# Fillers, later weight steps and a moved factor in a hand-planned kernel

## The chip, the cores and the metric

One Trainium2 chip, one core of it. The metric is the device time of one execution in microseconds; lower is better.

## What is computed

Three stages follow each other: a gated linear attention in chunks, and two feed-forward blocks. Cut to what matters:

```python
# 1. attention: batch 4, 8 heads, 768 steps, head size 32, state size 16
y = (C B^T * decay, causal) @ x  +  decay * (C @ state)          # per chunk
# 2. tokens as rows: 3072 x 256
xn = x / sqrt(mean(x * x) + 1e-6) * rms_g
g = xn @ w_gate; x = (g * sigmoid(g) * (xn @ w_val)) @ w_out     # 256 -> 1536 -> 256
# 3.
h = x @ w_in; solu = h * softmax(h)                              # 256 -> 1024
out = (layernorm(solu) * g_ln) @ w_out2                          # 1024 -> 256
```

All of it is float32. The kernel splits each operand of the large products in a high and a low part of type fp32r and adds three products (high x high, low x high, high x low).

## The kernel before

The 3072 tokens are 24 units `u` of 128 tokens and 6 blocks `b` of four units. A unit goes through the attention; a block through the gated stage in 12 steps `f` of 128 columns; a unit again through the last stage.

**One unit of attention.** TensorE builds the decay matrix for units 0 to 3 (`lpe`, L259; later units load it, L227) and `pcb` = B C (L301). ScalarE takes exponentials (L267), POOL masks (L271), VectorE multiplies both into `L` (L307) and prepares `cd` (L250) and `xb` (`bw`, L231). TensorE makes `y` (old state through L321, the unit's own part L326, new state L331). VectorE copies the state (L340, L342) and spreads it (`sbd`, L348); the next unit's `y` needs it. Then comes the normalisation: ScalarE squares `y` (`sq`, L355) and copies it (`xc`, L389), TensorE sums the squares (`ms`, L361), VectorE scales the sum (`ts`, L374), POOL takes the power -1/2 (`pw`, L379), TensorE spreads the factor over 128 columns of the same PSUM tile (`rb`, L383), VectorE multiplies copy, weight `rms_g` and factor (`xn`, L394), ScalarE makes the high part (`xh`, L401), VectorE the low part (`xl`, L405). A block's first gate product needs the low parts of all its four units.

**One step of the gated stage.** TensorE computes gate and value (`gm`, `vm`, six matmuls each, L558), ScalarE the tanh (L572), VectorE two products (L576, L580), ScalarE the high part `ah` (L586), VectorE or POOL the low part `al` (L592), TensorE adds into the output (`o0`, `o1`, L600).

**Weights.** 26 pieces arrive as 512 KB of 64-bit words (float64 bits). VectorE turns each into float32 in three steps (`wc`, L116, L119, L122); ScalarE makes the high part (`wh`, L129), VectorE or POOL the low part by a subtraction (`w`, L133). Pieces 0 to 17 go, three by three (gate, value, output), to two steps `f` each of block 0.

**What sets the order.** `plan()` places every operation `op(name, engine, us, due, fn, after, new, use)` in one list by rule: for each engine it takes, of the operations that could start within a slack of the earliest, the one that is due first. `us` and due times are written numbers. `new` and `use` count tiles in rings of fixed size, `alt` lets POOL take an operation of VectorE. The engines then run their part of the list in order and wait for each other by semaphores. Accesses of one PSUM tile by different engines are kept in the order of the list. Constants: `PRO` is when block 0 is planned to start, `FIRST` the least length of block 0, `Y0` when the first four units are due and how far apart, `SLACK0` and `SLACK` the slack before and after `PRO + 8`, `CROW` when the cumulated decays are due, `HLAG` how late the last stage of a block is due. Loads are issued by SyncE in the order of the list.

Of the kernel before, what the change touches and what calls it, by code (L numbers as in the profile page):

```python
# [11 lines left out]
AF = mybir.ActivationFunctionType  # L12
ALU = mybir.AluOpType
AX = mybir.AxisListType

P = 128
# [12 lines left out]
PRO = 34.0  # L29
FIRST = 63.0  # L30
VIA_PE = ()
WARM = 7
Y0 = (9.0, 4.0)
YPOS, YSPAN = 0.65, 1.0
TAILGAP = 5.0
SLACK = 0.1
SLACK0 = 0.1
# [3 lines left out]
MARGIN = {"PE": 0.5}  # L41
CROW = 30.0
WGAP = 8.0
HLAG = (50.0, 26.0)
# [7 lines left out]
def fused_kernel(ctx, tc, aT, xbt, bcT, wg, wv, wo1, rg, wi2, wo2, gl, consts, out):  # L52
    nc = tc.nc
    V, A, G, T, S = nc.vector, nc.scalar, nc.gpsimd, nc.tensor, nc.sync
# [143 lines left out]
    st = {}  # L198
# [187 lines left out]
    def at_xc(u):  # L386
        d = st[u]
        d["xts"] = sp.tile([P, 2, P], F32, name="xts", bufs=BUFS["xts"])
        A.activation(d["xts"], d["y"][:, 0:256].rearrange("p (g i) -> p g i", g=2), AF.Copy)  # L389

    def at_xn(u):
        d = st[u]
        for g in range(2):
            V.scalar_tensor_tensor(out=d["xts"][:, g], in0=d["xts"][:, g], scalar=rgt[:, g:g + 1],  # L394
                                   in1=d["y"][:, 384:512], op0=ALU.mult, op1=ALU.mult)
# [222 lines left out]
    ops = {}  # L618
# [70 lines left out]
    for u in range(NU):  # L689
# [62 lines left out]
        op(f"xc{u}", "ACT", 0.42, Y, (at_xc, u), after=[f"y{u}", f"sq{u}"], new=[("xts", f"xt{u}")], use=[f"y{u}", f"xt{u}"])  # L752
        op(f"xn{u}", "DVE", 0.6, Y, (at_xn, u), after=[f"rb{u}", f"xc{u}"], use=[f"y{u}", f"xt{u}"])
# [49 lines left out]
    for u in range(NU):  # L803
        b, k = unit_blk[u]
        n = blk[b][1]
        if b + 1 < NB:
            lag = [HLAG[min(q, 1)] for q in (b, b + 1)]
            H = start[b + 1] + lag[0] + k * (start[b + 2] - start[b + 1] + lag[1] - lag[0]) / n
        else:
            H = start[NB] + 14 + TAILGAP * k  # L810
# [93 lines left out]
    for u in range(2):  # L904
        ops[f"sbd{u}"]["after"].append("cst")
        ops[f"xn{u}"]["after"].append("cst")

    early = [f"lpe{u}.{g}" for u in range(NPE) for g in range(2)] + ["e1p"] + ["cr0", "cr1"]
    ops["wh22"]["after"] += early + ["sf"]

    def plan():
# [48 lines left out]
        while len(order) < len(ops):  # L960
            best = None
            dve = None
            for e, names in ready.items():
                if e == "POOL":
                    names = names + [nm for nm in ready["DVE"] if "alt" in ops[nm] and nm != dve]
                c = [(est(ops[nm], e, MARGIN.get(e, 0.0) if free[e] > PRO else 0.0), nm) for nm in names]
# [14 lines left out]
            if e != o["e"]:  # L981
                o = ops[nm] = dict(o, us=o["alt"][0], fn=o["alt"][1])
                ready["DVE"].remove(nm)
            else:
                ready[e].remove(nm)
            order.append((t, nm))
# [24 lines left out]
    with tc.manual_schedule():  # L1011
# [21 lines left out]
        for _, nm in seq:  # L1033
            fn, *a = ops[nm]["fn"]
            fn(*a)
# [64 lines left out]
```

## Time and profile before

| | |
|---|---|
| time, median of 3 runs | 563.78 us (561.93 to 565.23) |
| the profiled execution | 565.08 us, its span 563.4 us |
| TensorE busy | 546.5 us, 97% of the span |
| VectorE, ScalarE, POOL busy | 390.9, 290.3, 84.8 us |
| chain that ended last | TensorE 81%, VectorE 15%, DMA 2% |

The shares are means over stages. How to read the rows further down: times are microseconds from the start of the span; a matmul of float32 appears as two records; "PEclk" is the granted clock of TensorE as a share of 2.4 GHz (0.50 is 1.2 GHz); "idle before" an instruction is what its engine stood still, with the engine and line that ended it.

### The profile page before, as it was taken

Reading aid. Unit: us, or ns where it says so; the run is one execution under the profiler, and the core shown is the slowest. Engines: PE = TensorE matmul, PEld = TensorE weight load, DVE = VectorE, ACT = ScalarE, POOL = GpSimd, SP = SyncE. Lnnn points to the kernel's source line nnn. Section 1 sums busy time; section 2 is a strip of 40 time slices with the busy share of each in tenths; the row PEclk is TensorE's granted clock in tenths of the full one; section 3 lists DMA queues with packets and bytes.
Section 4 is the critical chain, followed back from the end, with each engine's and each line's share of the span. In section 5 each row is a group of like instructions: output and inputs, shape, how many; then the busy total and the mean of one; then the engine's idle time right before and its main releaser. Section 6 shows DMA issues by size and latency. Waiting matters only on the chain.

```text
span 563.4 us, 9443 instructions
## 1 busy us (share of the span) xinstructions
PE 546.5 (97%) x3544; PEld 461.1 (82%) x3544; DVE 390.9 (69%) x789; ACT 290.3 (52%) x654; POOL 84.8 (15%) x118
## 2 busy tenths in 40 slices
PE   9879998899999999999999999999999999999996
PEld 8757886687888888888888888888888888888795
DVE  5788999999876776575684574684674574564763
ACT  6437654666555564463474454554543353343464
POOL 2333323212221010110111100110100000000010
PEclk9579999999999999999999999999999999999999
DMA  7464765542022021121120220220200000000000
GB/s 213 132 212 140 216 203 194 182 145 71 14 72 76 2 80 47 43 72 36 54 76 11 75 70 10 80 70 10 72 2 9 10 1 9 11 1 10 9 20 30
DMA packets 44366, 39.33 MB, mean 70 GB/s; under 512 B 3936, under 2 KB 36896, under 8 KB 44320
## 3 DMA queue, kind: packets, MB, share of 16 engines
q1 hardware_dynamic: 44320, 38.72, 22.5%
q8 instruction: 28, 0.46, 0.4%
q14 instruction: 18, 0.15, 0.1%
HBM read 35.37 MB, written 3.34 MB: 69 GB/s over the span
## 4 chain that ended last, share of the span: by engine, by line
PE 81%; DVE 15%; DMA 2%; issue 1%; ACT 1%; SPq 0%; POOL 0%; DVEq 0%; ACTq 0%; POOLq 0%
PE pv L558 15%; PE pg L558 15%; PE po L600 14%; PE ph L436 12%; PE pf L538 12%; PE pt L514 4%; PE pcb L301 3%; DVE wt L119 2%; PE y L326 2%; DVE wt L122 2%; DVE th L580 2%; PE y L321 1%; DVE al L592 1%; DVE th L576 1%; DVE L L307 1%; DVE wt L116 1%
## 5 line engine op out<-in xcount | busy, mean ns | idle before, releaser
L586 ACT ACTIVATE ah<-th 128x512 fp32r<-128x512 f32 x72 | 45.2, 628 | 52.2 <-PE po L600 38.8
L580 DVE TENSOR_TENSOR th<-pv,th 128x512 f32<-128x512 f32 x72 | 49.8, 691 | 29.2 <-PE pv L558 24.1
L592 DVE TENSOR_TENSOR al<-th,ah 128x512 fp32r<-128x512 f32 x70 | 49.3, 704 | 26.0 <-ACT ah L586 25.6
L576 DVE SCALAR_TENSOR_TENSOR th<-th,pg 128x512 f32<-128x512 f32 x72 | 49.1, 682 | 20.0 <-ACT th L572 19.7
L558 PE MATMUL pg<-xh,wg_h 128*128 128x512 f32 x144 | 59.5, 413 | 2.3 <-ACT xh L401 1.2
L600 PE MATMUL po<-ah,wo_h 128*128 128x512 f32 x144 | 60.3, 419 | 0.0
L600 PE MATMUL po<-al,wo_h 128*128 128x512 f32 x144 | 56.7, 394 | 2.3 <-DVE al L592 2.3
L558 PE MATMUL pv<-xh,wv_h 128*128 128x512 f32 x144 | 58.4, 406 | 0.0
L558 PE MATMUL pg<-xh,wg_l 128*128 128x512 f32 x144 | 57.0, 396 | 0.0
L558 PE MATMUL pg<-xl,wg_h 128*128 128x512 f32 x144 | 56.8, 394 | 0.0
L600 PE MATMUL po<-ah,wo_l 128*128 128x512 f32 x144 | 56.7, 394 | 0.0
L558 PE MATMUL pv<-xl,wv_h 128*128 128x512 f32 x144 | 56.5, 392 | 0.0
L558 PE MATMUL pv<-xh,wv_l 128*128 128x512 f32 x144 | 56.4, 392 | 0.0
L572 ACT ACTIVATE th<-pg 128x512 f32<-128x512 f32 x72 | 42.6, 592 | 26.6 <-PE pg L558 26.4
L502 POOL TENSOR_TENSOR sc<-sc,mhalf 128x1 f32<-128x1 f32 x24 | 14.1, 587 | 263.6 <-DVE sc L497 263.6
L237 ACT ACTIVATE L<-L,cneg 128x128 f32<-128x128 f32 x160 | 50.5, 390 | 0.6 <-DMA L<-crow 0.6
L460 ACT ACTIVATE ut<-ph,sc 128x1024 f32<-128x1024 f32 x20 | 22.3, 1116 | 54.5 <-DVE sc L447 54.5
L538 PE MATMUL pf<-wo_h,uth 128*128 128x256 f32 x176 | 49.6, 282 | 0.3 <-DVE utl L528 0.2
L538 PE MATMUL pf<-wo_h,utl 128*128 128x256 f32 x176 | 49.6, 282 | 0.0
L538 PE MATMUL pf<-wo_l,uth 128*128 128x256 f32 x176 | 49.5, 281 | 0.0
L447 DVE TENSOR_REDUCE sc<-ph 128x1 f32<-128x1024 f32 x20 | 24.5, 1225 | 31.7 <-PE ph L436 31.7
L523 ACT ACTIVATE uth<-pt 128x512 fp32r<-128x512 f32 x44 | 26.0, 595 | 31.1 <-PE pt L514 30.9
(138 smaller groups left out, 1225.2 us busy)
## 6 DMA issues: line engine op xcount, KB each, us to landing
L<-crow SPq DMA_DIRECT2D x20, 512.0 KB
stage<-in_wo_dram SPq DMA_DIRECT2D x10, 512.0 KB
xb<-in_xbt_dram SPq DMA_DIRECT2D x24, 192.0 KB
stage<-in_wg_dram SPq DMA_DIRECT2D x6, 512.0 KB
bc<-in_bcT_dram SPq DMA_DIRECT2D x48, 64.0 KB
stage<-in_wv_dram SPq DMA_DIRECT2D x6, 512.0 KB
out_dram<-ob SPq DMA_DIRECT2D x24, 128.0 KB
stage<-in_wi_dram SPq DMA_DIRECT2D x4, 512.0 KB
```

Of the source, the lines that this page charges most:

```text
L237: A.activation(d["L"][:, h], d["L"][:, h], AF.Exp, bias=cneg[:, u * 8 + h:u * 8 + h + 1])
L436: T.matmul(ph[c], xx[:, kk, k * P:(k + 1) * P], ww[:, kk, 512 * c:512 * c + 512], start=(i == 0), stop=(i == 5))
L447: V.tensor_reduce(out=sc[:, 0:1], in_=ph[0], axis=AX.X, op=ALU.max, negate=True)
L523: A.activation(d["uT"][0][:, 4 * c:4 * c + 4].rearrange("p k t -> p (k t)"), d["ptc", c], AF.Copy)
L538: T.matmul(d["pf"][:, 0:DM], uu[:, k], ww[:, k], start=(k == 0 and i == 0), stop=(k == 7 and i == 2))
L558: T.matmul(ps[:, :n], ww[:, kk, f * P:(f + 1) * P], xx[:, kk, :n], start=(i == 0), stop=(i == 5))
L572: A.activation(d["th"], d["pg"], AF.Tanh, scale=0.5)
L576: V.scalar_tensor_tensor(out=d["th"], in0=d["th"], scalar=1.0, in1=d["pg"], op0=ALU.add, op1=ALU.mult)
L580: V.tensor_tensor(out=d["th"], in0=d["pv"], in1=d["th"], op=ALU.mult)
L586: A.activation(d["ah"], d["th"], AF.Copy)
L592: e.tensor_tensor(out=d["al"], in0=d["th"], in1=d["ah"].bitcast(F32), op=ALU.subtract)
L600: T.matmul(po[b, m][:, :n], ww[:, f, m * P:(m + 1) * P], aa, start=(f == 0 and i == 0), stop=(f == NF - 1 and i == 2))
```

## The change

Three edits of code and seven of constants. `xc` takes the weight `rms_g` as the scale of ScalarE's copy, in two instructions, one for each half (each half has its own weight column); `xn` becomes one product of 128x256 on VectorE, and waits no longer for the weight's load, `xc` does. In the planner, TensorE's margin (an operation of another engine counts as ready that much later) becomes a function `mg`: weight operations get a margin of 1.0 us on every engine (names that begin with `w` but for `wd`), TensorE's others keep 0.5 after `PRO`. And `warm` puts matmuls of the constant `ones` into 62 unused columns of the last `y` tile wherever TensorE is planned to be idle for over 0.5 us before `PRO + 6`, in a number that fills 70% of that time. The constants move the due times, so the whole list is ordered anew.

```diff
-PRO = 34.0
-FIRST = 63.0
+PRO = 28.0
+FIRST = 70.0
-Y0 = (9.0, 4.0)
+Y0 = (9.0, 3.5)
-SLACK = 0.1
-SLACK0 = 0.1
+SLACK = 0.05
+SLACK0 = 0.2
-CROW = 30.0
+CROW = 20.0
-HLAG = (50.0, 26.0)
+HLAG = (40.0, 26.0, 1)
+WMG = 1.0
+FILL = 0.7
...
     def at_xc(u):
         d["xts"] = sp.tile([P, 2, P], F32, name="xts", bufs=BUFS["xts"])
-        A.activation(d["xts"], d["y"][:, 0:256].rearrange("p (g i) -> p g i", g=2), AF.Copy)
+        for g in range(2):
+            A.activation(d["xts"][:, g], d["y"][:, g * P:(g + 1) * P], AF.Copy, scale=rgt[:, g:g + 1])
     def at_xn(u):
-        for g in range(2):
-            V.scalar_tensor_tensor(out=d["xts"][:, g], in0=d["xts"][:, g], scalar=rgt[:, g:g + 1],
-                                   in1=d["y"][:, 384:512], op0=ALU.mult, op1=ALU.mult)
+        V.tensor_tensor(out=d["xts"], in0=d["xts"], in1=d["y"][:, 384:512].unsqueeze(1).to_broadcast([P, 2, P]), op=ALU.mult)
...
+    def warm(u, n):
+        if u not in st:
+            return
+        for _ in range(n):
+            T.matmul(st[u]["y"][:, 322:384], ones, ones[:, 0:62], start=True, stop=True, skip_group_check=True)
...
+        def mg(nm, e):
+            if nm[0] == "w" and nm[1] != "d":
+                return WMG
+            return MARGIN.get(e, 0.0) if free[e] > PRO else 0.0
...
-                c = [(est(ops[nm], e, MARGIN.get(e, 0.0) if free[e] > PRO else 0.0), nm) for nm in names]
+                c = [(est(ops[nm], e, mg(nm, e)), nm) for nm in names]
...
+            if e == "PE" and lasty is not None and t < PRO + 6 and t - free[e] > 0.5:
+                order.append((free[e], (warm, lasty, int((t - free[e]) * FILL / 0.22))))
```

The planned `us` of `xc` and `xn` change places (0.42 and 0.6). The formula around `HLAG` gives 40 for block 0 and 26 for the others, where it gave 50 and 26.

In the rows of order below each line is an instruction (line, operation, output<-inputs, shape); lines of the changed kernel are numbered anew. ScalarE behind the exponentials of unit 1, before:

```order
L267 ACTIVATE L<-pv,cneg 128x128 x4
L129 ACTIVATE wv_h<-wt 128x2x256
L355 ACTIVATE sq<-y 128x256
L389 ACTIVATE xts<-y 128x256
L267 ACTIVATE L<-pg,cneg 128x128 x4
```

and now:

```order
L269 ACTIVATE L<-pv,cneg 128x128 x4
L357 ACTIVATE sq<-y 128x256
L392 ACTIVATE xts<-y,rgt 128x128 x2
L269 ACTIVATE L<-pg,cneg 128x128 x4
L269 ACTIVATE L<-pv,cneg 128x128 x4
L402 ACTIVATE xh<-xts 128x2x128
L357 ACTIVATE sq<-y 128x256
L392 ACTIVATE xts<-y,rgt 128x128 x2
L131 ACTIVATE wv_h<-wt 128x2x256
```

The high part `wv_h` of weight piece 1 moved from ahead of unit 0's square to behind unit 1's copies.

TensorE from the fourth unit's `y` to block 0's first product, before (the first `rb` is unit 2's):

```order
L326 MATMUL y<-L,xb 32x128 x8
L331 MATMUL y<-xb 32x64 x4
L383 MATMUL y<-ident,r 128x128
L361 MATMUL y<-ones,sq 128x1 x2
L383 MATMUL y<-ident,r 128x128
L558 MATMUL pg<-xh,wg_h 128x512
```

and now:

```order
L328 MATMUL y<-L,xb 32x128 x8
L333 MATMUL y<-xb 32x64 x4
L917 MATMUL y<-ones 128x62 x2
L363 MATMUL y<-ones,sq 128x1 x2
L917 MATMUL y<-ones 128x62 x4
L385 MATMUL y<-ident,r 128x128
L559 MATMUL pg<-xh,wg_h 128x512
```

Unit 2's `rb` moved ahead of this piece; the two groups of L917 are all the fillers of the program.

VectorE from unit 3's scaled sum to its low part, before:

```order
L374 TENSOR_SCALAR r<-y 128x1
L122 SCALAR_TENSOR_TENSOR wt<-stage,wt 128x512
L116 TENSOR_SCALAR wt<-stage 128x512
L119 SCALAR_TENSOR_TENSOR wt<-stage,wt 128x512
L394 SCALAR_TENSOR_TENSOR xts<-xts,rgt,y 128x128 x2
L133 TENSOR_TENSOR wv_l<-wt,wv_h 128x2x256
L405 TENSOR_TENSOR xl<-xts,xh 128x2x128
```

and now:

```order
L376 TENSOR_SCALAR r<-y 128x1
L118 TENSOR_SCALAR wt<-stage 128x512
L121 SCALAR_TENSOR_TENSOR wt<-stage,wt 128x512
L124 SCALAR_TENSOR_TENSOR wt<-stage,wt 128x512
L396 TENSOR_TENSOR xts<-xts,y 128x256
L135 TENSOR_TENSOR wg_l<-wt,wg_h 128x2x256
L406 TENSOR_TENSOR xl<-xts,xh 128x2x128
```

Before, the steps between were the last of piece 4 and two of piece 5; now they are the three of piece 4, and the subtraction is piece 3's.

## Rows read from the trace of the kernel before

**Rows 1.** Chain of waits, 9 to 48 us: start, us, engine, what, line.

```profile
7.96 4.25 DMA cd<-in_bcT_dram
...
13.35 1.06 DVE wt L119
...
15.16 0.03 ACT wv_h L129
...
16.36 0.24 DVE s L340
...
17.66 1.92 PE pv L259 x8
...
22.06 2.01 PE pcb L301 x16
...
40.22 2.96 PE pg L558 x6
```

**Rows 2.** Stretches, TensorE alone: from:to, length, busy, clock, DMA share, GB/s.

```profile
16.00:17.00 1.00, 0.36 (x2) 0.82 0.67 120
30.00:30.50 0.50, 0.50 (x20) 0.71 0.00 0
37.00:38.00 1.00, 0.00 (x0) 0.56 1.05 402
43.50:44.00 0.50, 0.50 (x3) 0.55 1.05 331
```

**Rows 3.** Timeline of the prologue: start, us, engine, line, operation, idle before.

```profile
10.77 1.06 PE L259 MATMUL pv<-um,la 128*128 128x128 f32 x8
...
11.99 1.16 ACT L267 ACTIVATE L<-pv,cneg 128x128 f32<-128x128 f32 x4
...
16.64 1.01 PE L361 MATMUL y<-ones,sq 128*128 128x1 f32 x4 [1.95 <-DVE s L340]
...
21.21 0.44 PE L331 MATMUL y<-xb 128*32 128x64 f32 x8
...
30.27 0.30 PE L331 MATMUL y<-xb 128*32 128x64 f32 x8
...
34.49 0.29 PE L331 MATMUL y<-xb 128*32 128x64 f32 x6
...
35.61 0.60 PE L361 MATMUL y<-ones,sq 128*128 128x1 f32 x4 [0.58 <-ACT xts L389]
```

**Rows 4.** Groups by shape: count, then busy us, mean ns, idle before.

```profile
L119 DVE SCALAR_TENSOR_TENSOR wt<-stage,wt 128x512 int32<-128x512 int32 x26 | 19.5, 749 | 0.5
L394 DVE SCALAR_TENSOR_TENSOR xts<-xts,rgt,y 128x128 f32<-128x128 f32 x48 | 14.4, 341 | 6.3 <-PE y L383 6.2
L405 DVE TENSOR_TENSOR xl<-xts,xh 128x256 fp32r<-128x256 f32 x24 | 10.4, 435 | 2.9 <-ACT xh L401 2.8
L133 DVE TENSOR_TENSOR wg_l<-wt,wg_h 128x512 fp32r<-128x512 f32 x3 | 2.0, 682 | 0.0
L379 POOL TENSOR_TENSOR r<-r,mhalf 128x1 f32<-128x1 f32 x24 | 14.7, 614 | 78.2 <-DVE r L374 70.2 <-DMA xb<-in_xbt_dram 8.0
L389 ACT ACTIVATE xts<-y 128x256 f32<-128x256 f32 x24 | 9.2, 382 | 8.8 <-DVE s L342 6.2 <-DVE s L340 2.5
```

**Rows 5.** Stretch of 10 us: busy of PE, PEld, DVE, ACT, POOL, then clock.

```profile
100.00:110.00 10.00, 9.50 (x53) 7.31 (x51) 9.90 (x22) 5.86 (x15) 1.51 (x2) 1.00 0.74 231
```

**Rows 6.** Timeline of TensorE, 84 to 150 us, with idle before in brackets.

```profile
95.75 0.50 PE L600 MATMUL po<-al,wo_h 128*128 128x512 f32 x1 [1.84 <-DVE al L592]
...
106.72 0.50 PE L600 MATMUL po<-al,wo_h 128*128 128x512 f32 x1 [0.49 <-DVE al L592]
...
111.87 0.50 PE L558 MATMUL pg<-xh,wg_h 128*128 128x512 f32 x1 [0.98 <-DVE th L576]
...
135.53 0.35 PE L361 MATMUL y<-ones,sq 128*128 128x1 f32 x2 [0.20 <-DVE sq L369]
```

**Rows 7.** Timeline of VectorE: the tenth low part of block 0.

```profile
95.02 0.68 DVE L592 TENSOR_TENSOR al<-th,ah 128x512 fp32r<-128x512 f32 x1
```

More of the change, by code (lines that the diff above doesn't have):

```diff
@@ L751, in fused_kernel @@
         op(f"rb{u}", "PE", 0.12, Y, (at_rb, u), after=[f"pw{u}"], use=[f"y{u}"])
-        op(f"xc{u}", "ACT", 0.42, Y, (at_xc, u), after=[f"y{u}", f"sq{u}"], new=[("xts", f"xt{u}")], use=[f"y{u}", f"xt{u}"])
-        op(f"xn{u}", "DVE", 0.6, Y, (at_xn, u), after=[f"rb{u}", f"xc{u}"], use=[f"y{u}", f"xt{u}"])
+        op(f"xc{u}", "ACT", 0.6, Y, (at_xc, u), after=[f"y{u}", f"sq{u}"], new=[("xts", f"xt{u}")], use=[f"y{u}", f"xt{u}"])
+        op(f"xn{u}", "DVE", 0.42, Y, (at_xn, u), after=[f"rb{u}", f"xc{u}"], use=[f"y{u}", f"xt{u}"])
         op(f"xh{u}", "ACT", 0.42, Y, (at_xh, u), after=[f"xn{u}"] + ([f"xh{u-1}"] if k else []), new=[("xs", f"xs{b}")] if k == 0 else [],
@@ L806, in fused_kernel @@
         if b + 1 < NB:
-            lag = [HLAG[min(q, 1)] for q in (b, b + 1)]
+            lag = [HLAG[0] + (HLAG[1] - HLAG[0]) * min(1.0, q / HLAG[2]) for q in (b, b + 1)]
             H = start[b + 1] + lag[0] + k * (start[b + 2] - start[b + 1] + lag[1] - lag[0]) / n
@@ L905, in fused_kernel @@
         ops[f"sbd{u}"]["after"].append("cst")
-        ops[f"xn{u}"]["after"].append("cst")
+        ops[f"xc{u}"]["after"].append("cst")
     early = [f"lpe{u}.{g}" for u in range(NPE) for g in range(2)] + ["e1p"] + ["cr0", "cr1"]
     ops["wh22"]["after"] += early + ["sf"]
+    def warm(u, n):
[3 more added lines that the diff above has]
+            T.matmul(st[u]["y"][:, 322:384], ones, ones[:, 0:62], start=True, stop=True, skip_group_check=True)
     def plan():
@@ L958, in est @@
             return t
-        while len(order) < len(ops):
+        def mg(nm, e):
+            if nm[0] == "w" and nm[1] != "d":
+                return WMG
+            return MARGIN.get(e, 0.0) if free[e] > PRO else 0.0
+        lasty = None
+        while len(end) < len(ops):
             best = None
@@ L985, in plan @@
                 ready[e].remove(nm)
+            if nm[0] == "y":
+                lasty = int(nm[1:])
+            if e == "PE" and lasty is not None and t < PRO + 6 and t - free[e] > 0.5:
+                order.append((free[e], (warm, lasty, int((t - free[e]) * FILL / 0.22))))
             order.append((t, nm))
@@ L1033, in fused_kernel @@
         for _, nm in seq:
-            fn, *a = ops[nm]["fn"]
+            fn, *a = ops[nm]["fn"] if isinstance(nm, str) else nm
             fn(*a)
```

## Prediction

> **What bounds the kernel now.** I read the busy time by stretches first, then the chain of waits up to block 0, then the timeline of TensorE. The reader should see three stages. Late in the span TensorE is the bound (97% busy over all), and nothing in the change touches a matmul there; the last 140 TensorE entries stand in the same order in both programs. Up to 40.22 us four units of attention run one after the other, and block 0's first product can only start behind the fourth [rows 1]. Between, from about 45 to 140 us, VectorE is the tight engine: in 100 to 110 us it is busy 9.90 of 10 us, TensorE 9.50 [rows 5]. TensorE's waits in that stage are 1.84, 0.49, 0.98 and 0.20 us, together 3.51, the first three for VectorE [rows 6]. So an earlier block 0 is worth only what VectorE, with its weight steps, can follow.
>
> The chain to 40.22 us has two faults [rows 1]. First, a load of `cd` takes 4.25 us to land behind a weight piece, VectorE stands for it, and then ScalarE's `wv_h` at 15.16 us stands ahead of unit 0's square; the squared sum of unit 0 (L361) comes at 16.64 us only [rows 3]. Second, TensorE's clock. It was idle for 1.95 us ahead of that, from 14.7 us [rows 3], and within 16 to 17 us the granted clock falls from 2.4 to 1.2 GHz; it comes back at 30.3 us. It falls again within 37 to 38 us and is back within 43.5 to 44 us [rows 2]. At 1.2 GHz the eight matmul records of L259 take 1.92 us and the sixteen of `pcb` 2.01 us [rows 1]; at 2.4 GHz the same eight took 1.06 us [rows 3].
>
> **The change, part by part: the prologue.** I walk unit by unit through the new order with the durations of the rows, at 2.4 GHz.
> Unit 0 to 1: `y` of unit 0 now stands ahead of unit 1's `pcb`, so it starts when L259 ends at 10.77 + 1.06 = 11.8 us [rows 3] and has its eight products and four state matmuls through by 12.6. VectorE's part before it is shorter, since unit 1's `bw` and `cd` go to POOL (whose next work waits for ScalarE until 12.1 anyway) and `cd`'s load is issued ahead of `wv`'s. ScalarE is busy with exponentials until 11.99 + 1.16 = 13.15 us [rows 3]; then square and the two weighted copies follow at once, `wv_h` later. The square costs a like step, 0.3. The copy was one instruction of 0.38 us [rows 4]; two of 128x128 cost a step of 0.26 (from the four in 1.16 us: three steps and one of 0.38) and 0.38, so 0.64, or 0.26 more per unit. L361 can start at 14.1 instead of 16.64 and takes 0.6 [rows 3]; two L259 groups of 1.0, the transposed factor 0.3 and `y` of unit 1 with 1.3 follow: it ends near 18.3, against 21.65 before [rows 3].
> Unit 1 to 2: the state copy behind a conversion step (0.75, L119 [rows 4]), square and copies 0.9, L361 0.6, two L259 groups 2.0, factor 0.3, `y` 1.3, handoffs 0.3: 24.4, against 30.57 [rows 3].
> Unit 2 to 3: copy, square and copies 1.7, L361 0.6, two `L` products on VectorE 1.4 (0.68 each, as L133 of that size [rows 4]), `y`'s products 1.1: 29.2, against 34.78 [rows 3].
> Unit 3 to block 0: state copy and ScalarE's three until 30.8. Here stand the fillers, the only six in the whole program. They write the tile `y` that VectorE and ScalarE read, so the first two wait for those reads and run behind the gap, not in it. A filler is bounded below by a 64-column matmul record (0.29 us for six, so 0.1 per filler with its two records) and above by L361, which has the same weight load: 0.60 for two matmuls, 0.3 each, doubled at 1.2 GHz [rows 3]. I take 0.25, nearest to L361. Two: 0.5, so L361 ends at 31.9 instead of 31.4; VectorE would be in a conversion step until then anyhow. The four before the factor: 1.0, beside POOL's 0.61 [rows 4] and beside three steps of weight piece 4, which now stand on VectorE between the sum and the factor's use (none over the 0.75 of L119, the first about 0.4: 1.9). Those steps set that place: 34.0; the fillers cost nothing under this cover at 2.4 GHz, and up to 0.7 at 1.2. Then the product 0.44, ScalarE's copy 0.42: block 0 starts near 35.2, against 40.22: **5.0 us earlier**. I keep 4 to 6 for it.
> The product itself was two instructions of 0.341 [rows 4] and is now one of 128x256; nearest is L405 of that shape, 0.435 [rows 4]: 0.25 less per unit on VectorE. In return ScalarE has 0.26 more; from unit 4 on it is covered, as ScalarE is busy 5.86 of 10 us [rows 5].
> The gap ahead of block 0 stays (29.2 to 35.2, with few matmuls), so I expect its first products at 1.2 GHz again, six in 2.96 us [rows 1]; nothing is won or lost there.
>
> **VectorE takes most of it back.** Counting the two orders up to the end of block 0's first `al`, the new one has done less: one piece's conversion (1.9), two `cd` and one `bw` products (about 1.0), four units' weighting (4 x 0.25), but one subtraction more (0.68): 3.1 to 3.2 us less by then. So of the 5.0 only 1.9 is idle time of VectorE saved. Up to the tenth `al` the lists hold the same work but for: subtractions of weights 12 instead of 8 (POOL takes four fewer), 4 x 0.682 = 2.7 more [rows 4]; seven units' weighting, 7 x 0.25 = 1.7 less; one `cd` product, 0.3 less. Together 0.7 more. The tenth `al` ended at 95.02 + 0.68 = 95.7 us [rows 7], the moment at which TensorE's 1.84 us wait ends [rows 6]. In the new order it ends at 95.7 + 0.7 - 1.9 = 94.5. TensorE, 5 us ahead, waits there some 4 us in all, in pieces from about 68 us on, as each subtraction of weight pieces 7 to 16 comes close behind its use. At that place it has one unit's attention matmuls more behind it (`pcb` 1.0, half of 2.01 [rows 1], and 1.6 for the rest) and six gate products fewer (half of 2.96 [rows 1]): 1.1 us of work more. So 1.2 + 1.1 = 2.3 us are won by then. The three later waits of before (1.67 us [rows 6]) should mostly go, for TensorE then trails VectorE by more; and POOL's four fewer subtractions leave VectorE freer (an L119 beside POOL took 1.05 us [rows 1] against the mean of 0.749 [rows 4]). I add 1.5 for both. **Sum: 3.8 us less.** The weight loads keep pace: piece 7's load now stands behind two 512 KB loads of `L`, but its first step stands at about 46 us, some 2 us behind where I put its landing; were it later, TensorE would lose as much.
>
> The profiled execution took 565.08 us, span 563.4 and 1.7 around it; it lies 1.3 above the median of the runs, 563.78. 565.1 - 3.8 = 561.3, and 1.3 lower for a median: **560.0**.
>
> **A rule against the trace.** The granted clock fell in the gap after 14.7 us, and again within 37 to 38 us although L361's four records had run at 35.61 us, after 0.58 us of idling [rows 2, 3]; so those few short matmuls did not hold it. The Trainium skill (TensorE: Matmul & The Clock Gate, section "HAM oscillation — how this bites in real kernels") puts the fall on waits between groups of matmuls that let the array go cold; read strictly, matmuls in the gap would keep 2.4 GHz. By the row the fillers do nothing, and the sum is as above; by the rule block 0 starts at full clock, which is rival C.
>
> **Rivals.**
> A, no change: the clock falls in the new prologue too. TensorE still idles there about 0.5 us at 13.6 and 1.0 at 19.2 (`pcb` done, ScalarE not). If one of these does it, L259, `y`, `pcb` and L361 of two units double: 4 to 5 us, block 0 at 40. VectorE idles 4.5 us longer than in my walk, so the tenth `al` ends at 99, 3.3 later than before; 1.1 of work ahead and the 1.5 come off, 0.7 are left: 564.5. For it: a gap of 1.95 did it before; against: these are shorter. Chance 0.19.
> B, slower: the same fall, but the clock does not come back before block 0 (before it needed until 30.3, and the new prologue has shorter dense stretches). Then unit 3's `y`, L361, the cumulated decays' matmuls and the fillers double too, 3 us more: block 0 near 43, the tenth `al` at 102, all of it behind rival A: 567.5. It decides when block 0 starts later than about 42. Chance 0.09.
> C, the fillers do hold the clock: six products take 1.5 instead of 2.96 and three more follow; VectorE has conversions as cover, so up to 1.8 us: 558.2. This is also the change doing what it says; my forecast says that six fillers behind their waits don't. Chance 0.07.
> D, VectorE follows: with POOL off its back its steps shrink and the 5.0 us come through whole, later waits included: 565.1 - 5.0 - 1.5 - 1.3 = 557.3. For it: L119's mean of 0.749 is 0.07 over L133 of the same size; against: 9.90 of 10 us busy. Chance 0.12.
> The forecast keeps 0.53, itself 558 to 562.5 by the 4 to 6 us and the 1.5 either way.
>
> **How the numbers follow.** 0.5% is 2.8 us, about what a measurement of this kernel can tell from no change; faster means below 561.0. Of the forecast's 0.53 I give 0.38 to that side, with C and D 0.57. Within 0.5%: 0.15 + 0.17 of A = 0.32; slower: B and the rest of A, 0.11. The range leaves out B and the lowest of D: 556.2 to 565.4.
>
> **What would show it.** Right: unit 1's square ahead of `wv_h`, L361 of unit 0 near 14.1 us, clock 2.4 GHz throughout 14 to 29 us, block 0's first product at 34 to 36.5 us and slow; the tenth `al` at 93 to 96 us; TensorE's waits from 65 to 95 us up to about 4 us, and few after. Wrong: a granted clock of 1.2 GHz before 29 us (A, B), fillers between the fourth `y` and its sum with a fast first product (C), no wait on VectorE from 65 to 95 us (D), or a first product past 38 us at full clock, which would mean that my walk misses a wait.

## The result, and the profile after

The changed kernel takes **565.68 us** (median of 20 runs, 564.05 to 568.91); the kernel before, run beside it, 563.77 (560.80 to 565.46). The ratio is 1.0052, with a 95% interval of 1.0034 to 1.0069: slower by half a per cent, 1.9 us. The forecast was 560.0 with a range up to 565.4, so it was wrong in size and in sign.

The profiled execution took 565.36 us, span 563.6, which is level with the one of before (565.08, span 563.4). It lies 0.3 below its median; that of before lay 1.3 above its own. A comparison of the two traces alone would read "no change".

TensorE's timeline of the prologue, after (start, us, engine, line, operation, idle before it), answers to [rows 3]:

```profile
13.45 0.61 PE L363 MATMUL y<-ones,sq 128*128 128x1 f32 x4 [0.18 <-ACT xts L392]
...
18.27 0.29 PE L333 MATMUL y<-xb 128*32 128x64 f32 x8
...
21.55 0.60 PE L363 MATMUL y<-ones,sq 128*128 128x1 f32 x4 [1.89 <-ACT xts L392]
22.02 2.05 PE L261 MATMUL pg<-um,la 128*128 128x128 f32 x8
23.86 1.81 PE L261 MATMUL pv<-um,la 128*128 128x128 f32 x8
...
33.49 0.66 PE L917 MATMUL y<-ones 128*128 128x62 f32 x4 [2.06 <-ACT xts L392]
33.99 0.56 PE L363 MATMUL y<-ones,sq 128*128 128x1 f32 x4
34.87 1.26 PE L917 MATMUL y<-ones 128*128 128x62 f32 x8 [0.32 <-DVE r L376]
35.92 0.42 PE L385 MATMUL y<-ident,r 128*128 128x128 f32 x1
38.04 0.79 PE L559 MATMUL pg<-xh,wg_h 128*128 128x512 f32 x1 [1.70 <-ACT xh L402]
```

The reader is to see that the front of the prologue goes as the walk said (unit 0's sum at 13.45, unit 1's `y` done at 18.56), and that from there it loses. Unit 1's sum waits 1.89 us, the two L261 groups behind it take 2.05 and 1.81 instead of 1.1 each, and the fillers (L917) run behind their waits. Block 0 starts at 38.04, against 40.22 [rows 1]: 2.2 us earlier, not 5.0.

The granted clock of the stretches in which it falls or rises, after, answers to [rows 2] (from:to, length, then busy time of PE, PEld, DVE, ACT and POOL, granted clock, DMA share, GB/s):

```profile
21.00:22.00 1.00, 0.45 (x4) 0.45 (x5) 0.83 (x2) 1.00 (x3) 0.00 (x0) 1.00 0.88 180
22.00:23.00 1.00, 1.00 (x6) 1.00 (x6) 0.74 (x3) 0.01 (x1) 0.49 (x1) 0.51 0.57 147
25.00:26.00 1.00, 1.00 (x9) 1.00 (x8) 0.18 (x1) 0.54 (x3) 0.63 (x1) 0.79 0.06 16
35.00:36.00 1.00, 1.00 (x9) 1.00 (x9) 0.88 (x2) 0.00 (x0) 0.88 (x2) 0.83 0.95 312
42.00:43.00 1.00, 1.00 (x5) 0.73 (x4) 0.36 (x1) 0.15 (x1) 0.00 (x0) 0.75 0.98 379
```

TensorE goes from 2.4 to 1.2 GHz within 22 to 23 us, behind the idle 1.89 us, and is back within 25 to 26; it falls again within 35 to 36, behind the idle 2.06 us and while the fillers run, and is back within 42 to 43.

The chain of waits of after, 12 to 40 us, names what came ahead of unit 1's sum and of unit 3's normalisation (start, us, what):

```profile
12.23 5.76 DMA xb<-in_xbt_dram
...
18.01 0.77 DVE xb L233
18.78 0.33 DVE xts L396
...
31.95 2.92 DMA cd<-in_bcT_dram
...
35.09 0.44 DVE wt L118
35.55 0.89 DVE wt L121
36.46 0.69 DVE wt L124
37.15 0.34 DVE xts L396
```

The chain gives a load the whole time from issue to landing; what VectorE stood still for it, its timeline says:

```profile
14.54 0.43 DVE L118 TENSOR_SCALAR wt<-stage 128x512 int32<-128x512 int32 x1 [1.62 <-DMA stage<-in_wv_dram]
...
18.01 0.77 DVE L233 TENSOR_TENSOR xb<-xb,wdec 128x128 f32<-128x128 f32 x1 [0.46 <-DMA xb<-in_xbt_dram]
...
20.29 0.27 DVE L344 SCALAR_TENSOR_TENSOR s<-s,e,y 128x64 f32<-128x64 f32 x1
```

The load of `xb` takes 5.76 us to land, but VectorE stands only 0.46 us for it, and 1.62 us earlier on for the load of weight piece 1. Then the weighting (L233), unit 0's product (L396), a `cd` product and two conversion steps run before unit 1's state copy (L344), although unit 1's `y` was done at 18.56. The second load of the chain, at 31.95, held VectorE for 0.27 us (before the step at 35.09); the three conversion steps of weight piece 4 then run ahead of unit 3's normalisation.

VectorE's tenth low part of block 0 and the wait of TensorE on it, after, answer to [rows 6, 7]:

```profile
96.97 0.68 DVE L593 TENSOR_TENSOR al<-th,ah 128x512 fp32r<-128x512 f32 x1
...
97.71 0.51 PE L601 MATMUL po<-al,wo_h 128*128 128x512 f32 x1 [1.49 <-DVE al L593]
```

It ends at 97.65 us, 1.95 **later** than before, although block 0 started 2.2 earlier. And TensorE, from block 0's first product to the end, as one stretch with the same columns, before:

```profile
40.22:563.40 523.18, 513.41 (x3258) 431.33 (x3258) 363.95 (x726) 270.84 (x600) 71.10 (x95) 1.00 0.20 62
```

and after:

```profile
38.04:563.60 525.56, 514.86 (x3258) 431.88 (x3258) 364.85 (x719) 278.30 (x621) 63.08 (x85) 0.99 0.20 61
```

Busy time is +1.45 us and idle time 10.70 against 9.77, so +0.93: together 2.4, which is the 2.2 won by the start and 0.2 more. About 0.4 of the 1.45 is the clock: ten products of block 0 run 0.43 us apart here before the clock is back, and eight before, where 0.23 is usual later.

**A ledger of VectorE.** Since the tenth low part is where the forecast put its sum, I add up VectorE's timeline to its end: *idle* is time between steps; *stretch* is time by which a step lasts longer than is usual for its operation and shape (the lower quartile over the traces of this case; counted where it is over 0.08 us); *work* is the rest. Stretch and work depend on that choice of the usual length by up to 0.4 us; idle does not.

| | ends | idle | stretch | work |
|---|---|---|---|---|
| before, tenth `al` | 95.70 | 15.54 | 3.99 | 76.17 |
| after, tenth `al` | 97.65 | 16.27 | 5.29 | 76.09 |
| before, fifteenth | 125.03 | 16.21 | 3.99 | 104.83 |
| after, fifteenth | 129.59 | 16.88 | 6.24 | 106.47 |

The forecast had work +0.7, idle -1.9 and no row for stretch. To the tenth `al` work came as -0.1, idle as +0.7 and stretch as +1.3: of the error of 3.15 us idle is 2.6 and stretch 1.3, and work takes 0.8 back.

### The profile page after: what moved, and what is told of

It is laid out like the page before. It is cut to its first block, busy times and chain, and to the rows that moved or that the text cites. A ratio compares the mean times of both kernels' runs of the same rounds, so it can differ in the third digit from the quotient of the medians.

```text
span 563.6 us, 9460 instructions
## 1 busy us (share of the span) xinstructions
PE 544.1 (97%) x3556; PEld 458.1 (81%) x3556; DVE 390.2 (69%) x774; ACT 298.1 (53%) x678; POOL 76.4 (14%) x109
## 4 chain that ended last, share of the span: by engine, by line
PE 76%; DVE 17%; issue 2%; DMA 2%; POOL 1%; ACT 1%; DVEq 0%; POOLq 0%; ACTq 0%
PE pv L559 14%; PE pg L559 14%; PE po L601 14%; PE pf L539 12%; PE ph L437 11%; PE pt L515 4%; PE pcb L303 3%; DVE wt L121 2%; DVE th L581 2%; DVE al L593 2%; DVE th L577 2%; PE y L328 2%; DVE wt L124 2%; DVE wt L118 2%; DVE L L309 1%
## 5 line engine op out<-in xcount | busy, mean ns | idle before, releaser
L471 DVE SCALAR_TENSOR_TENSOR ut<-ph,ut 128x1024 f32<-128x1024 f32 x20 | 24.5, 1225 | 23.9 <-ACT ut L461 23.9
```

Of the source, the lines that this page charges most:

```text
L471: V.scalar_tensor_tensor(out=d["u"], in0=ph[0], scalar=1.0, in1=d["u"], op0=ALU.mult, op1=ALU.mult, accum_out=sc[:, 2:3])
```

## The experiments

**Theories.** Theory 1: VectorE's list sets the pace to about 140 us, so an earlier block 0 is worth only what VectorE's idle time shrinks by. Theory 2: TensorE's clock in the prologue sets the time. Theory 3: one part of the change has a price of its own. A fourth came up on the way: VectorE's stretched steps are held up by POOL.

### One part at a time

No fillers:

```
-FILL = 0.7
+FILL = 0.0
```

> The changed kernel without its six filler products, all else as it is. In the profiled execution of the changed kernel the fillers stood at 33.49 us (0.66) and 34.87 us (1.26), both behind a wait, so unit 3's factor came about 1 us later than it could. Theory 1 (VectorE's list paces up to about 140 us): block 0 starts up to 1 us earlier (first product near 37) but the time stays at 565.0 to 565.9 us, ratio 1.002 to 1.004. Theory 2 (the clock's falls in the prologue set the time): without fillers the clock falls no more and no less, so 565 to 566 too, or up to 1 us worse if the fillers did hold it in some executions. Theory 3 (one part has its own price, here the fillers): back by the 1 us that they cost or more, 563.8 to 564.7.

566.19 us, ratio 1.0047 (1.0024 to 1.0069). The six fillers neither cost nor give anything that can be measured; in its profile block 0 started at 38.96 and the clock fell in the prologue too (0.50 from 20 to 24 us).

The weight in ScalarE's copy alone, on the kernel before:

```
-        A.activation(d["xts"], d["y"][:, 0:256].rearrange(...), AF.Copy)
+        for g in range(2):
+            A.activation(d["xts"][:, g], d["y"][:, g * P:(g + 1) * P], AF.Copy, scale=rgt[:, g:g + 1])
...
+        V.tensor_tensor(out=d["xts"], in0=d["xts"], in1=d["y"][:, 384:512].unsqueeze(1).to_broadcast(...), op=ALU.mult)
```

> The kernel before with only the weight moved into ScalarE's copy (two copies with a scale, one product on VectorE instead of two); all lists in their old order. VectorE saves about 0.27 us per unit (two steps of 0.341 against one of 0.41). Theory 1: seven units lie ahead of 100 us, 1.7 to 1.9 us less on VectorE, and its waits shrink by about that: 562 to 563 us, ratio 0.9965 to 0.9985. Theory 2: the clock's falls are not touched (the gap of 1.95 us ahead of unit 0's squared sum stays): 563.8, ratio 0.999 to 1.001. Theory 3, that this part is the one with the price: ScalarE's second copy lengthens each unit's chain by 0.25 us, 564.5 to 566.

563.80 us, ratio 0.9999 (0.9978 to 1.0019). VectorE did 1.7 us less work up to the tenth `al` (74.44 against 76.17), as costed, and nothing that can be measured reached the end; theory 1's gain of 0.15 to 0.35% is at best its small end.

The converse, the changed kernel with the old copy and products:

> The changed kernel with the copy and the two products on VectorE of before (the list as in the changed kernel). VectorE has 0.27 us more per unit, seven units by 100 us: theory 1 expects the tenth al 1.5 to 1.9 later and 566.5 to 567.5 us. Rival (the weight in the copy gives nothing, as on the kernel before alone, 563.8): 565.3 to 566.

565.46 us, ratio 1.0038 (1.0017 to 1.0059). The rival came true: this part is worth nothing that can be measured, on either list.

The margin on weight steps alone, on the kernel before:

```
+        def mg(nm, e):
+            if nm[0] == "w" and nm[1] != "d":
+                return 1.0
+            return MARGIN.get(e, 0.0) if free[e] > PRO else 0.0
...
-                c = [(est(ops[nm], e, MARGIN.get(e, 0.0) if free[e] > PRO else 0.0), nm) for nm in names]
+                c = [(est(ops[nm], e, mg(nm, e)), nm) for nm in names]
```

> The kernel before with only the margin of 1 us on the readiness of weight steps in the planner; constants, copies and products as before. VectorE makes two subtractions more (16 instead of 14; POOL's is the rest of 23). Theory 1: 2 x 0.68 = 1.4 us more on VectorE up to the end of the weights, less what a rarer stall behind a load gives: 564 to 565.5, ratio 1.000 to 1.003. Theory 2: nothing, 563.8. Theory 3, that this part is the one with the price: the whole 1.9 us, 565 to 566.5.

**568.75 us**, ratio 1.0093 (1.0062 to 1.0125): 5 us slower, far more than either theory had, and that with block 0 starting at 36.59, 3.6 us *earlier* than in the profile of before. This run refuted two things at once, that an early block 0 is a gain by itself and that the clock is the price (mean granted clock of the profiled execution 0.991, before 0.981). The groups by shape of VectorE between 45 and 140 us show where it went (count, then busy us, mean ns, idle before); before first:

```profile
L119 DVE SCALAR_TENSOR_TENSOR wt<-stage,wt 128x512 int32<-128x512 int32 x19 | 14.3, 751 | 0.2
L122 DVE SCALAR_TENSOR_TENSOR wt<-stage,wt 128x512 int32<-128x512 int32 x19 | 14.0, 735 | 0.3
```

and with the margin alone:

```profile
L122 DVE SCALAR_TENSOR_TENSOR wt<-stage,wt 128x512 int32<-128x512 int32 x20 | 17.8, 888 | 0.2
L119 DVE SCALAR_TENSOR_TENSOR wt<-stage,wt 128x512 int32<-128x512 int32 x20 | 17.0, 850 | 0.4
```

The same steps on the same data last 100 to 150 ns longer in the mean. By the ledger to the fifteenth `al` (134.72, before 125.03): idle -0.2, work +3.9 (its list has more weight steps ahead of that place), stretch 9.97 against 3.99, +6.0. (The trace has 17 subtractions on VectorE instead of 13, four more and not the two that were expected.)

Margin and copy with the old constants and without fillers:

```
-PRO = 28.0
+PRO = 34.0
...
-FILL = 0.7
+FILL = 0.0
```

(`FIRST`, `Y0`, `SLACK`, `SLACK0`, `CROW` and `HLAG` go back in the same way.)

> The changed kernel with the planner's constants of before (start of block 0, its length, first unit, slacks, row of the decays, lag) and no fillers, so margin on weights and weight in the copy alone. VectorE makes 21 subtractions here, as in the changed kernel (before 14). Theory 1: 7 x 0.68 = 4.8 us more and 16 x 0.27 = 4.3 less on VectorE: near before, 563.5 to 565. Theory 2: depends on the clock: with a fall ahead of 20 us as before, 564 to 566; without it 562 to 563. Theory 3, that the constants are the part with the price: 563.5 or less.

564.54 us, ratio 1.0014 (0.9993 to 1.0035). Theory 1's number came out; theory 3's 563.5 lies at the edge of the interval. With the copy's new costs the planner makes quite another list of the same margin, with a stretch of 4.63 to the fifteenth `al` instead of 9.97: so the margin has no fixed price; it seems to lie in the list that falls out of it.

### Is it the number of subtractions on VectorE?

By the traces the changed kernel makes 19 of its 22 subtractions of weight pieces on VectorE, the kernel before 13; POOL does the others. Six of them given to POOL in the changed kernel, then to VectorE in the kernel before, the order of both lists kept:

```
+        for i in (1, 3, 8, 9, 15, 20):
+            ops[f"w{i}"]["fn"] = (w_lo, i, G)      # in the other run V
```

> The changed kernel with the subtractions of weight pieces 1, 3, 8, 9, 15 and 20 on POOL, as in the kernel before, instead of on VectorE; the list else the same. That takes 6 x 0.68 = 4.1 us off VectorE, four of the six ahead of the tenth al, and gives POOL steps of some 1.2 us. Theory 1 (what VectorE has to do up to about 140 us sets the time, so the seven subtractions that moved to it are the price): the tenth al ends 1.5 to 2.7 us earlier than 97.65, the median falls to 563.5 to 564.5. Rival (the price is in the order of the list, not in VectorE's work): 565 to 566.5, with TensorE waiting for POOL's late subtractions.

569.81 us, ratio 1.0104 (1.0069 to 1.0138): wrong way round for theory 1. The tenth `al` ends at 100.53: work -2.3, but stretch +2.4 and idle +2.9. Its steps beside subtractions on POOL hold 3.7 us of the stretch, where in the changed kernel they hold 0.9.

> The kernel before with the same six subtractions on VectorE instead of POOL; the list else the same. Theory 1: 4.1 us more on VectorE up to 110 us, less what POOL's slower step kept others waiting: the tenth al 1.5 to 2.7 us later than 95.70, the median 565.3 to 567. Rival (the order is the price, not VectorE's work): 563.5 to 564.5.

564.25 us, ratio 1.0016 (1.0001 to 1.0031). Five more subtractions ahead of the tenth `al` make 2.75 us more work, and it ends only 0.42 later: stretch fell from 3.99 to 2.16 and idle by 0.5. A subtraction on POOL can come back as stretch, then, as in the run before; here, though, none of the eight subtractions that POOL makes ahead of the tenth `al` of the kernel before stretched a step, and what fell away (3.8 to 1.9 us) is stretch beside POOL's selects (the masking of `L`), which met other VectorE steps in the shifted list. My form of theory 1, by which VectorE's instruction count is the price, fell here.

### POOL holds VectorE up

One place of many, in the kernel before: the timeline of VectorE,

```profile
65.64 1.59 DVE L122 SCALAR_TENSOR_TENSOR wt<-stage,wt 128x512 int32<-128x512 int32 x1
```

and that of POOL:

```profile
65.36 1.32 POOL L241 TENSOR_SCALAR_AFFINE_SELECT L<-L 128x1024 f32<-128x1024 f32 x1 [2.55 <-ACT L L237]
```

POOL's step runs to 66.68. The conversion that started inside it lasts 1.59 instead of 0.68 us: 0.91 more, and 1.04 of it lay beside POOL. It looks held until POOL is done and then runs nearly its usual time (0.55 us). Two runs test that, with 24 products of a constant on POOL that nobody needs, and with as much of POOL's time in fills that read nothing:

```
+            if nm in DUMMY:               # second conversion step of pieces 7 to 18
+                for _ in range(2):
+                    G.tensor_tensor(out=scr, in0=um, in1=um, op=ALU.mult)
...
+                for _ in range(5):        # the control
+                    G.memset(scr, 1.0)
```

> The kernel before with 24 products on POOL that nobody needs (128x384 of a constant in SBUF, written to a tile of their own; two behind the second conversion step of each of the weight pieces 7 to 18), all else the same. New theory (POOL holds up VectorE): in the trace of before the VectorE steps that read two SBUF tensors, or convert from SBUF, last up to 1.6 instead of 0.7 us where they start beside a long POOL step; the sixteen long POOL steps between 45 and 140 us stretch them by 3.7 us in all, 0.23 each. 24 more of about 1 us then cost 4 to 6 us of VectorE and, as VectorE sets the pace, 567 to 570 us. Rival (VectorE's order and waits are the price, POOL's company is harmless): 563.5 to 565.

**573.88 us**, ratio 1.0188 (1.0158 to 1.0218): 10.6 us slower, more than expected. The tenth `al` ends at 104.83, 9.1 later: idle 15.33, work 75.99, both as before, and stretch 13.51 against 3.99.

> The control: the same places, but POOL only fills the tile with a constant (five fills of 128x384 at each place instead of two products), reading nothing from SBUF. New theory: the two-tensor steps of VectorE are not held up; what is left is that POOL's own steps come up to 2 us later: 563.5 to 565.5 us. If POOL's being busy at all were the price (its own steps coming late), this would cost as much as the products, 567 or more.

562.54 us, ratio 1.0001 (0.9977 to 1.0025): nothing, though POOL was busy as long. The same three VectorE steps stand beside the products and beside the fills. With the products, the timeline of VectorE:

```profile
61.77 0.41 DVE L116 TENSOR_SCALAR wt<-stage 128x512 int32<-128x512 int32 x1
62.10 1.31 DVE L592 TENSOR_TENSOR al<-th,ah 128x512 fp32r<-128x512 f32 x1
63.34 1.31 DVE L119 SCALAR_TENSOR_TENSOR wt<-stage,wt 128x512 int32<-128x512 int32 x1
```

and POOL beside them:

```profile
61.77 2.33 POOL L1040 TENSOR_TENSOR scr<-um 128x384 f32<-128x384 f32 x2
```

With the fills, VectorE:

```profile
56.67 0.69 DVE L116 TENSOR_SCALAR wt<-stage 128x512 int32<-128x512 int32 x1
57.28 0.67 DVE L592 TENSOR_TENSOR al<-th,ah 128x512 fp32r<-128x512 f32 x1
57.88 0.68 DVE L119 SCALAR_TENSOR_TENSOR wt<-stage,wt 128x512 int32<-128x512 int32 x1
```

and POOL:

```profile
56.66 2.49 POOL L1040 MEMSET scr<- 128x384 f32 x5
```

Steps that take two tensors from SBUF are held by POOL's reads (1.31 against 0.67 and 0.68) and not by its fills; the conversion's first step, with one tensor, is held by fills that started just ahead of it (0.69 against 0.41). It is held by selects as well. In the changed kernel, VectorE:

```profile
64.92 1.32 DVE L118 TENSOR_SCALAR wt<-stage 128x512 int32<-128x512 int32 x1
```

and POOL:

```profile
64.66 1.29 POOL L243 TENSOR_SCALAR_AFFINE_SELECT L<-L 128x1024 f32<-128x1024 f32 x1 [4.25 <-DMA stage<-in_wo_dram]
```

Over the 18 traces, 33 of the 34 such first steps that started inside a select lasted longer. Steps that take one operand from PSUM kept their length: none of the 980 that started inside a POOL step lasted longer by over 0.08 us. One of them in the kernel before, beside a subtraction of 1.30 us on POOL from 91.00:

```profile
91.03 0.68 DVE L576 SCALAR_TENSOR_TENSOR th<-th,pg 128x512 f32<-128x512 f32 x1
```

The Trainium skill says this in "SBUF — State Buffer", section "Who interferes with whom": VectorE and GpSimd share a port pair that one instruction holds whole, and a VectorE instruction with two SBUF inputs meets it against a GpSimd instruction that reads SBUF, not against one that only writes. These runs agree for steps with two tensors (1.31 against 0.67 and 0.68). The held one-tensor step (1.32 instead of 0.42) is beyond what that rule says.

### How much of it is the clock

Fillers that run in the gaps, on a tile that nobody reads any more, in the changed kernel and in the kernel before:

```
-            T.matmul(st[u]["y"][:, 322:384], ones, ones[:, 0:62], ...)
+            T.matmul(pcs[u][1][:, 3], ones, ones, ...)       # unit u's pcb, read by then
+FILLS = {"ms1": 5, "ms3": 6, "rb3": 4, "gm0.0": 5}          # after: how many ahead of which step
+FILLS = {"ms0": 6, "ms3": 2, "rb3": 7, "gm0.0": 4}          # before
```

> The changed kernel with its six fillers replaced by twenty 128x128 ones that write a tile nobody reads any more, so that they run in the gaps and not behind them: five ahead of unit 1's squared sum, six ahead of unit 3's, four ahead of unit 3's factor, five ahead of block 0. If matmuls in the gaps hold the clock (theory 2), the granted clock stays at 2.4 GHz, the ten first products of block 0 take 0.23 instead of 0.43 us each, 2 us less, and unit 2's L261 groups 1.0 instead of 2.0: 562 to 563.5 us. Theory 1 (VectorE's list paces to about 140 us): the clock may hold and block 0 start near 36, but the tenth al still ends at 97 to 98 and the time stays at 565 to 566.5. If the gaps' fillers don't hold the clock, the falls stand where they stood, within 22 to 23 and 35 to 36 us.

564.28 us, ratio 1.0006 (0.9989 to 1.0024). The profiled execution still fell once, from 21 to 28 us, behind a gap of 1.88 us that I had left without fillers. Its first product came at 40.01, **2 us later** than in the profile of after, and its tenth `al` at 97.87, only 0.2 later: so the start of block 0 is not what counts there. VectorE's idle time is what stayed with it, 16.66 against 16.27.

> The kernel before with nineteen fillers in its gaps, written to a tile nobody reads any more: six in the gap of 1.95 us ahead of unit 0's squared sum, two ahead of unit 3's, seven ahead of unit 3's factor, four ahead of block 0. Order and work else as before. If they hold the clock: no fall within 16 to 30 us, block 0's first product near 36 instead of 40.22, and its products at full clock. Theory 2 then expects 559.5 to 561.5 us, theory 1 (VectorE's list paces) 562.5 to 564, with VectorE's tenth al at 94 to 95.5. If they don't hold it: 563.5 to 565.

**562.25 us**, ratio 0.9974 (0.9960 to 0.9988): faster than both kernels. Timeline of TensorE at the gap that began the fall in the kernel before:

```profile
14.96 1.50 PE L916 MATMUL pcb<-ones 128*128 128x128 f32 x12
17.23 0.61 PE L364 MATMUL y<-ones,sq 128*128 128x1 f32 x4 [0.77 <-DVE s L343]
```

The stretches that follow, with the columns of the stretches above:

```profile
15.00:20.00 5.00, 4.23 (x55) 3.83 (x53) 4.17 (x9) 3.33 (x11) 3.03 (x3) 1.00 0.64 179
20.00:25.00 5.00, 4.19 (x42) 3.76 (x42) 5.00 (x14) 2.85 (x10) 2.74 (x4) 1.00 0.66 186
25.00:30.00 5.00, 3.93 (x54) 3.31 (x53) 4.64 (x11) 2.47 (x8) 2.71 (x3) 1.00 0.46 157
35.00:40.00 5.00, 4.44 (x21) 3.18 (x21) 4.96 (x11) 1.83 (x4) 0.40 (x1) 1.00 1.06 329
```

Fillers in the gaps keep 2.4 GHz all through the prologue. Behind it the clock still falls once, where TensorE stands 1.84 us for VectorE's tenth `al`:

```profile
90.00:95.00 5.00, 3.50 (x10) 2.82 (x11) 4.28 (x8) 1.75 (x3) 0.00 (x0) 0.75 0.38 107
```

VectorE's idle time up to the tenth `al` falls to 10.17 and that `al` to 91.44, 4.3 earlier, against a profiled execution of before that ran some 20 of its first 44 us at 1.2 GHz [rows 2]; against the medians 1.5 us are left.

Fillers and copy together on the kernel before:

> The kernel before with the nineteen fillers in its gaps and with the weight in ScalarE's copy, order else as before. The fillers alone gave 562.25 us with the tenth al at 91.44. Theory 1: 0.27 us less per unit on VectorE, so the tenth al at 90 and 561 to 562 us, ratio 0.995 to 0.998. Rival (the weight in the copy gives nothing): 562.0 to 562.5.

562.15 us, ratio 0.9972 (0.9953 to 0.9990): the copy adds nothing here either.

The list of margin and copy with old constants, and the changed kernel with its own, both with 22 fillers in all their gaps:

> The changed kernel with the constants of before and with 22 fillers in the prologue's gaps, on a tile nobody reads any more (without them 564.54 us, the clock falling between 20 and 27 us and again from 36 us). If the clock holds, as with the fillers in the kernel before (-1.5 us): 562.5 to 563.5. If VectorE takes it back, since its idle time in the prologue shrinks by less than block 0 gains: 564 to 565.

**561.94 us**, ratio 0.9977 (0.9958 to 0.9996), mean granted clock 1.000.

> The changed kernel, its own constants kept, with the same 22 fillers in the prologue's gaps as the run on old constants (561.94 us): with the clock held in both, what is left between them is the constants. If the constants are a price (block 0 taken as longer, other slacks, the earlier lag): 563 to 564.5, with VectorE's tenth al at 94.5 to 97. If the changed kernel's loss was the clock's falls alone: 561.5 to 562.5, level with the run on old constants, and the tenth al near 93.

563.28 us, ratio 0.9986 (0.9969 to 1.0003), clock 0.997. Against the changed kernel (1.0034 to 1.0069) the fillers win 2.4 us, and the intervals don't touch. With the clock held in the prologue of all three, before takes 562.25, margin and copy 561.94, and the new constants 563.28; the intervals overlap. The clock of the single runs says more. At a mean of 1.000 the new constants take 562.2 in the mean (four runs) and the old ones 562.1 (nine): the same. The new constants' higher median comes from eight runs at 0.992 to 0.998, in which the clock still falls somewhere; in the profiled one it is 0.69 from 95 to 100 us, behind a wait of 1.48 us for VectorE's tenth `al`. So these two runs show no price of the constants where the clock holds; which of them leads to the later fall was not tried.

### Less work for VectorE

Without the second conversion step of the weight pieces 6 to 25:

```
+        elif c == 1 and i >= 6:
+            pass
```

> The changed kernel without the second conversion step of weight pieces 6 to 25 (twenty steps of about 0.75 us on VectorE, 15 us in all; the sign bit of those weights is left out of the result), order else the same. Theory 1 (VectorE's list paces): TensorE's waits of 3.9 us between 50 and 150 go, and an earlier block 0 comes through to the end: 559 to 561 us, and as far below the same cut in the kernel before as block 0 starts earlier, 1 to 2 us. Theory 3 (the price lies on TensorE itself or in the tail, not on VectorE): also faster, but still 1 to 2.5 us above the cut kernel before.

> The kernel before without the same twenty conversion steps (the sign bit of those weights is left out of the result). Theory 1: its waits of 4.3 us between 50 and 150 go: 559.5 to 561 us. Theory 3: the same here; the two part on the changed kernel with this cut, which theory 1 puts 1 to 2 us below this one, and theory 3 1 to 2.5 above.

560.17 (ratio 0.9936, 0.9914 to 0.9959) and 559.74 us (0.9921, 0.9894 to 0.9948). Both gain, 5.5 and 4.0 us of the 15 taken away: VectorE's work does set part of the pace. With VectorE relieved the difference of the medians shrinks from 1.9 to 0.4, with intervals that overlap. Each time lies in theory 1's range, but the difference on which the theories part fits neither. Nor is the shrinking sure: at a mean clock of 0.988 or 0.989 the changed kernel with this cut took 560.7 (one run), the kernel before 558.0 and 559.6. So it is shown that VectorE's work matters in both kernels, and not that the 1.9 us are lost there.

## Why the prediction was wrong, point by point

**The frame held.** VectorE is the tight engine up to some 140 us, and the worth of an earlier block 0 is what VectorE's idle time shrinks by. The runs bear that out: in the prologues whose block 0 started at 36.59 and 40.01 the start told nothing of the time (568.75 and 564.28). The work term, costed at 0.7 more, came out as -0.1.

**The sum, term by term.** The tenth `al` was to end 1.2 us earlier and ended 1.95 later: 3.15 us of error, and the step that failed (its parts, idle and stretch, follow below). Behind it the forecast had 1.1 + 1.5 = 2.6 us to win; from there to the end of the span the profiled executions took 467.70 and 465.95 us, so 1.75 were won and 0.85 are missing. And the forecast took over the 1.3 us by which the profile of before lay above its median, where that of after lay 0.3 below: 1.6. Together that is 5.6 of the 5.7 us between 560.0 and 565.68.

**The walk to 35.2 failed at unit 1.** Up to `y` of unit 1 it was within 0.7 us (13.45 for 14.1, 18.56 for 18.3). Then it put one conversion step of 0.75 us ahead of unit 1's state copy, which so came at about 19.05. It came at 20.29: VectorE had stood 1.62 us for weight piece 1 and 0.46 us for unit 2's `xb`, the weighting of that `xb` lasted 0.77 instead of 0.28 us beside a select on POOL, and four more steps stood behind it in the queue. The prediction followed the two products that moved to POOL, and not VectorE's own queue. Unit 1's sum so came at 21.55 instead of about 20.0, behind the gap of 1.89 us; the clock fell, and the L261 groups took 3.5 us together instead of 2.0. At the end of unit 2's `y` the walk was 2.5 us short (26.91 for 24.4), and at block 0 2.8 (38.04 for 35.2).

The walk had read the chain of the kernel before in the same way: of the 4.25 us of the load of `cd` there [rows 1] it says that VectorE stood for it. VectorE ended its step before at 12.13 and started on `cd` at 12.23, so it stood 0.1 us.

**One execution of before was taken for the kernel.** The 5.0 us were counted from 40.22. But where the clock falls in the prologue, and for how long, differs between executions of one program. In the run with fills on POOL, whose first fill started at 36.53, block 0 started at 36.29; in five others with the order of before up to there at 38.06, 39.37, 40.22, 40.59 and 40.72. With the order of after it was 37.21, 37.31, 38.04, 38.46 and 38.96. The runs show the same in the times. Over the 121 runs of before that list a clock, 29 with a mean granted clock below 0.983 took 565.6 in the mean, and 33 at 0.990 or 0.991 took 562.2. So the profiled execution of before, at 0.981, was one of the late ones, and the change had much less to win in the prologue than its trace showed. At nearly the same clock, 30 runs of before at 0.987 or 0.988 took 563.9 and six of after at 0.989 took 565.4; 21 of before at 0.984 took 563.9 and five of after at 0.983 or 0.985 took 566.9. The changed kernel is 1.5 to 3.0 us behind at like clock, so a lower mean clock does not explain the 1.9 us.

**"1.9 us of idle time saved" was -0.7.** That is the term which decides the sign. In executions with the prologue of before (15.54, 14.72, 15.04, 15.33 and 10.60) and of after (16.27, 17.73, 14.55, and 19.13 with subtractions on POOL), VectorE idled about as long in the new prologue or longer, up to the tenth `al`.

**"POOL's fewer subtractions leave VectorE freer", +1.5, had the wrong sign.** The row of 1.06 us beside POOL [rows 1] was read rightly as POOL's doing, but the POOL step there is a select (L271, 13.22 to 13.85 us), no subtraction. What counts is *which* VectorE step starts inside *which* POOL step. Beside the eight subtractions that POOL makes ahead of the tenth `al` of before, VectorE happened to start only steps that kept their length, so there was nothing to win. Of the stretch there all but some 0.5 us lies beside selects, and their number, 13, stays the same. The new list has six subtractions fewer on POOL and yet 1.3 us more stretch by the tenth `al` and 2.25 by the fifteenth. TensorE's waits from 65 to 95 us, put at 4, were 0.17, 0.29 and 0.26, since it had no such lead; those between 100 and 180 us, which were to go, shrank from 2.45 to 1.60, so 0.85 of the 1.5 came.

**The rivals.** A's mechanism, the clock falling in the new prologue, came true at 22 us, behind an idle 1.89 us, not at 13.6 or 19.2; and its numbers came nearest (tenth `al` at 99 for 97.65, 564.5 for 565.68); but with the clock held in the prologue (563.28) the changed kernel still isn't ahead of before with the same done to it (562.25). B's point, a block 0 later than 42, was never reached: slower came without it. C was half right: the six fillers as written hold nothing, fillers that run inside the gaps do (1.00 from 15 to 40 us in the kernel before). The rule of the Trainium skill weighed there ("TensorE: Matmul & The Clock Gate", section "HAM oscillation — how this bites in real kernels") puts the fall on waits between groups of matmuls; those rows agree with it. D fell.

**What is settled and what is not.** Shown: POOL steps that read SBUF hold up VectorE's steps on SBUF (573.88 against 562.54), that is worth microseconds here, and a clock held in the prologue is worth 1.5 us before and 2.4 after. Read from ledgers only, one execution each: that VectorE comes later by idle (+0.7), stretch (+1.3 to +2.3) and, at the fifteenth `al`, work (+1.6), of which part is made up later. Open: what the 1.9 us are in the end, which constant of the planner leads to the later waits, and about 1.0 of the 1.45 us of busy time that block 0's order costs TensorE itself.

## What to carry to other kernels

Where two engines share the pace, add up the second one's time as idle, stretch and work up to one named instruction: an earlier start of a stage that doesn't shrink the idle term was worth nothing here. Work moved to GpSimd cost VectorE nothing where it met steps with an operand in PSUM, and as fills; look at the longest rows of a shape, not at its mean, and at what GpSimd does beside them. The time from issue to landing in a chain of waits is no wait: the engine's own timeline has that (5.76 us against 0.46). And before counting from a stage whose clock falls, look at the clock of several executions: the one in the profile may be the slowest of them.

## What the runs showed of the hardware that I had not expected

- A VectorE step with two tensors in SBUF that starts inside a long GpSimd step that reads SBUF lasts until that step is over plus nearly its usual time: 1.59 and 1.55 instead of 0.68 us beside a select of 1.1 to 1.3, up to 1.78 beside a subtraction of 1.62. The conversion's first step, with one tensor, is held by a select too (1.32 instead of 0.42). Adding 24 GpSimd products of about 1.1 us cost 10.6 us; the same GpSimd time in fills cost nothing.
- The granted clock falls at different places in executions of one program, and 1% of mean granted clock goes with some 3 us: in the 121 runs of before, 565.6 us in the mean below 0.983 and 561.7 at 0.993.
- The gap ahead of unit 0's squared sum, which lost the clock for 14 us where TensorE idled in it, did not lose it with matmuls of no use in it; six matmuls placed behind the waits, as the change has them, did nothing (566.19 against 565.68 us).
